# Chunk 4's transposes moved behind the first FFN product

## The chip, the cores and the metric

The kernel runs on one core of a Trainium2 chip. A core has five engines that run side by side, each with its own list of instructions: TensorE (PE, matrix products), VectorE (DVE), ScalarE (ACT), GpSimd (POOL) and SyncE (SP, which here only issues transfers). The metric is the device time of one execution in microseconds; lower is better. Before the change four runs took 779.92, 779.97, 781.87 and 782.6 us, median 780.92.

## What is computed

The reference applies attention with decay (no softmax) and then a feed-forward network with three up-projections:

```python
scores = scale * np.matmul(q, k.transpose(0, 1, 3, 2))     # 8 batches, 8 heads, 576 tokens, head size 64
gamma = 1.0 - 2.0 ** (-5.0 - np.arange(H))
Dmat = np.where(rel >= 0, gamma[:, None, None] ** rel[None, :, :], 0.0)
ret = np.matmul(scores * Dmat, v)                          # then x = ret as (4608, 512)
h = np.maximum(np.maximum(x @ w1, x @ w2), x @ w3)         # w1, w2, w3: 512 x 768
out = h @ w_out                                            # 768 x 512
```

q, k and v are float32. The four weight matrices arrive as 64-bit floats, and the kernel itself turns their bits into float32.

## The kernel before

**Attention.** The 4608 tokens are 36 chunks of 128. For each chunk `load` fetches k, q and v; `decay_values` (POOL) multiplies v by the key decay; `transposes` brings k and q into the layout that the scores need; `scores` forms the products and masks them (DVE); `state` forms k times v for the running state; `keep` adds it to the state (DVE) and decays it (POOL); `values` forms the chunk's output from the masked scores and the old state (L296, L309), and `output` scales it on DVE into xT, the FFN's input (L184 in the profile). `values` also forms its chunk's kv product (L260) where it has not been formed yet. For chunks 0 to 6 `transposes` uses TensorE (L229) and copies the two results, kT and qT, out of PSUM on ScalarE (L231); later chunks use VectorE.

**FFN.** Four chunks make a tile of 512 tokens (CPT = 4), and there are nine tiles. The hidden size 768 is six blocks of 128. In tile 0 the up-projections are plain: nine units, one for each pair of blocks and each of w1, w2, w3. A unit has two products of four matmuls (L600), one per block. The first matrix's product is copied into h on ScalarE (L604), the others are joined by a maximum on DVE (L603). The first unit's first product is called fb0 below, its second fb1. Later tiles use a scheme with fewer products, whose sums need VectorE.

**Weights.** The weights come in 24 pieces of 128 x 512 (512 KB each), pieces 0 and 1 for the first unit, 2 and 3 for the second, and so on. `load_weights` issues the transfers on SP; six buffers hold the raw bits, and each finished piece issues the load of another into its buffer. `convert_all` is a generator, and `convert(n)` moves it on by n steps. A piece has four: a mask on DVE (L486) and the low word on ScalarE (L487); two exponent steps on ScalarE (L489, L492) and a mask on DVE (L491); L497 on DVE; L502 and L508 on DVE, the last of which writes the float32 weights. L489 needs L486, and L502 needs L492. Pieces 0 and 1 are worked one by one, later ones in pairs: masks of both, then products of both.

**Order of the work.** Nothing plans the order; it is the order in which the program emits it. Each engine takes its instructions in that order, and an instruction that waits holds up all behind it on its engine. The first four chunks are emitted ahead of the FFN of tile 0, with conversion steps between them. Then, for each tile, the FFN generator `ffn(t)` and the attention steps of the following tile, `steps(t + 1)`, take turns: during tile 0, slot 0 loads chunk 5, the first unit follows, slot 1 emits chunk 4's scores, state and keep, the second unit follows, slot 2 emits chunk 5's transposes, and so on. PSUM banks come from three small pools; `ps_r` has four banks in rotation, used by scores, kv products, the outputs from chunk 3 on and the transposes of chunks 4 to 6.

Of the kernel before, what the change touches and what calls it, by code (L numbers as in the profile page):

```python
# [79 lines left out]
def kernel(  # L80
# [23 lines left out]
    CPT = NT // C  # L104
# [45 lines left out]
    def start_of(g):  # L150
        r = -g * C % S
        return r if r < C else None
# [8 lines left out]
    raws, vds, qks, sts, states, kvs = {}, {}, {}, {}, {}, {}  # L161
# [12 lines left out]
    def chore(n=1):  # L174
        for _ in range(n):
            if urgent or chores:
                (urgent or chores).popleft()()  # L177

    def soon(step):

        if spread:
            urgent.append(step)
        else:
            step()  # L184
# [24 lines left out]
    def decay_values(g):  # L209
        t = vds[g] = vpool.tile([C, H, D], FP32, tag="vd", name="vd")  # L210
        nc.gpsimd.tensor_tensor(t[:], raws.pop(("v", g))[:], gk[:].unsqueeze(2).to_broadcast([C, H, D]),  # L211
                                op=ALU.mult)

    def pair(t, p):
        return t[:, 2 * p:2 * p + 2, :].rearrange("a h d -> a (h d)")

    def transposes(g):
        both = qks[g] = {}
        if g >= BY_PE:
            for n in ("k", "q"):  # L220
                t = both[n] = att.tile([P, NP, C], FP32, tag=n + "T", name=n + "T", bufs=2 if n == "k" else 3)
                soon(partial(nc.vector.transpose, t[:].rearrange("a p c -> a (p c)"),
                             raws.pop(("kx" if n == "k" else n, g))[:].rearrange("a p b i -> a (p b i)")))
            return
        for n, src in (("k", raws["k", g]), ("q", raws.pop(("q", g)))):
            pool, tag = (ps_r, "r") if g >= CPT else (ps_x, "x")
            pt = pool.tile([P, NP, C], FP32, tag=tag, name=n + "t")
            for p in range(NP):
                nc.tensor.transpose(pt[:, p, :], pair(src, p), ident[:C, :C])  # L229
            t = both[n] = att.tile([P, NP, C], FP32, tag=n + "T", name=n + "T", bufs=2 if n == "k" else 3)  # L230
            nc.scalar.copy(t[:], pt[:])  # L231
# [14 lines left out]
    def begins(g):  # L246
        return g + 1 < NG and start_of(g + 1) != 0

    def half(j):
        return slice(D * j, D * (j + 1))  # L250
# [12 lines left out]
    def keep(g):  # L263
        def step(t, kv):
            if start_of(g) is not None:
                nc.vector.tensor_tensor(t[:], kv[:], gs[:], op=ALU.mult)
            else:
                nc.vector.tensor_tensor(t[:], kv[:], states[g][:], op=ALU.add)  # L268
                nc.gpsimd.tensor_tensor(t[:], t[:], gs[:], op=ALU.mult)  # L269

        if begins(g):
            t = states[g + 1] = stp.tile([P, NP, D], FP32, tag="state", name="state")
            soon(partial(step, t, kvs[g]))
# [3 lines left out]
    def head(c, n):  # L277

        return NP * c + n

    def values(chunks, new_states=(), later=False):

        def before(g):
            return C if start_of(g) is None else start_of(g)

        chore(len(urgent))
        t, i = divmod(chunks[0], CPT)
        pool, tag = (ps_r, "r") if chunks[0] >= CPT - 1 else (ps_y, "y")  # L290
        o = [pool.tile([P, len(chunks), NP // 2, C], FP32, tag=tag, name="o") for _ in range(2)]
        for m, g in enumerate(chunks):
            for n in range(NP):
                for c in range(2):
                    h = head(c, n)
                    nc.tensor.matmul(o[n % 2][half(c), m, n // 2, :], lhsT=vds[g][:, h, :],  # L296
                                     rhs=sts[g][:, h % 2, h // 2, :], start=m == 0 and n < 2,
                                     stop=before(g) == 0, skip_group_check=True)
        for g in new_states:
            if g not in kvs:  # L300
                state(g)
        for m, g in enumerate(chunks):
            old = before(g)
            if old > 0:
                for n in range(NP):
                    for c in range(2):
                        h = head(c, n)
                        r = half(h % 2)
                        nc.tensor.matmul(o[n % 2][half(c), m, n // 2, :old], lhsT=states[g][r, h // 2, :],  # L309
                                         rhs=qks[g]["q"][r, h // 2, :old], start=False, stop=True,  # L310
                                         skip_group_check=True)
        finish = partial(output, chunks, o, t, i)
        if later:
            return finish
        finish()
        for g in new_states[:1]:
            if g >= CPT:
                keep(g)
# [220 lines left out]
    def late_room():  # L539
        pool = late["pool"]  # L540
        late["W"] = [pool.tile([P, NF, P], FP32, name=f"n{n}") for n in range(1, 9)]
        late["X"] = {n: pool.tile([P, NH], FP32, name=n)[:] for n in sorted({x[0] for x in X_SUMS})}
# [3 lines left out]
    def convert(n):  # L546
        for _ in range(n):
            next(converting, None)
# [48 lines left out]
    def up_plain(t, h, fb, i):  # L597
        ps = (ps_x, ps_y)[fb % 2].tile([P, NT], FP32, tag="xy"[fb % 2], name="up")
        for dc in range(NDC):
            nc.tensor.matmul(ps[:], lhsT=w_sb[i, fb][:, dc * P:(dc + 1) * P], rhs=xT[t][:, dc, :],  # L600
                             start=(dc == 0), stop=(dc == NDC - 1))
        if i > 0:
            return lambda: nc.vector.tensor_tensor(h[:, fb, :], h[:, fb, :], ps[:], op=ALU.max)  # L603
        return lambda: nc.scalar.copy(h[:, fb, :], ps[:])  # L604

    def ffn(t):

        h = hpool.tile([P, NF, NT], FP32, tag="h", name="h")
        if t == 0:
            for fp, i in units:  # L610
                for fb in (2 * fp, 2 * fp + 1):
                    maximum = up_plain(t, h, fb, i)
                    convert(4)
                    maximum()
                yield
            convert(6)
            for fb, _ in enumerate(downs_plain(t, h)):
                convert(4 if fb < 2 else 4 * len(pieces))
                if fb == 2:
                    while_converting.close()  # L620
                    late["pool"] = ctx.enter_context(tc.tile_pool(name="late", bufs=1))
                    late_room()
                    sums_of_outs()
                elif fb > 2:
                    chore(2)
                if fb in (1, 3):
                    yield
            yield
            return
        if t == 1:  # L630
            spread.append(True)
            weight_sums(0)
            weight_sums(2)
        plain = (2, 3) if t == 1 else ()
        order = (2, 3, 0, 1, 4, 5) if t == 1 else (0, 1, 4, 5, 2, 3)
        total = sum(24 if fb in plain else len(PRODUCTS) for fb in order)
        count = parts = 0
        for n, fb in enumerate(order):
            if fb not in plain:
                while fb // 2 not in summed_fp:  # L640
                    chore()
            steps_of_one = up_plain_all(t, h, fb) if fb in plain else up(t, h, fb)
            for step, cost in enumerate(steps_of_one):
                if fb in plain:
                    chore(8)
                elif step % 2 or step % 5 == 4:
                    chore(len(urgent) > 0)
                elif step % 4 == 2 and chores:
                    chores.popleft()()
                count += cost or 1  # L650
                if count * (NF // 2 * 3) >= (parts + 1) * total:
                    parts += 1
                    yield
            if n % 2:
                sums_of_hidden(h, fb // 2)
                if fb in plain:
                    weight_sums(fb // 2)
        chore(len(urgent))
        for n, _ in enumerate(downs(t, h)):
            chore(4)  # L660
            if n in (1, 3):
                yield
        yield

    def up_plain_all(t, h, fb):
        for i in range(3):
            up_plain(t, h, fb, i)()
            yield 8
# [36 lines left out]
    keep(2)  # L705
    convert(2)
    values([2], [2])
    transposes(4)
    convert(2)
    decay_values(4)  # L710
    values([3], [3])
    keep(3)
    convert(4)

    def steps(t):

# [95 lines left out]
```

## Time and profile before

One execution was profiled.

| | before |
|---|---|
| median of four runs | 780.92 us |
| time of the profiled execution | 781.87 us |
| its span, first to last instruction | 780.2 us |
| PE busy | 768.6 us (99%) |
| DVE busy | 568.7 us (73%) |
| ACT busy | 325.9 us (42%) |
| POOL busy | 102.7 us (13%) |
| mean granted PE clock | 0.998 |

Span and time differ by 1.67 us, which lies outside the first and last instruction. Times in the views are microseconds from the start of the span. In a timeline a row gives the start, the length, the engine, the line of the kernel and the tiles written and read; neighbouring instructions of one kind are merged, and the square brackets show how long the engine was idle before and what ended that. PE's float32 matmuls appear as two records each. A busy share averages over stages: what counts for an edit in the first 40 us is which wait ends last there.

### The profile page before, as it was taken

What the parts mean: (1) busy time and instruction counts of PE and PEld (TensorE: products, weight loads), DVE (VectorE), ACT (ScalarE), POOL (GpSimd) and SP (SyncE); (2) the same over time, 40 slices, a digit from 0 to 9 for tenths busy, and PEclk for the clock granted to TensorE, in tenths of its full rate; (3) what the DMA queues carried; (4) which work ended last, traced back from release to release, by engine and by line L of the source; (5) the groups of instructions that cost most, each with busy time, mean ns of one, the idle gap of its engine ahead of it and who ended that gap; (6) DMA issues with size and microseconds to landing.
All of it is one profiled execution on the core that took longest, in us unless ns stands there. A gap on an engine that the chain in (4) does not pass through costs nothing.

```text
span 780.2 us, 14439 instructions
## 1 busy us (share of the span) xinstructions
PE 768.6 (99%) x5000; PEld 625.6 (80%) x5000; DVE 568.7 (73%) x1248; ACT 325.9 (42%) x808; POOL 102.7 (13%) x124
## 2 busy tenths in 40 slices
PE   8899999999999999999999999999999999999998
PEld 6545545588888888888888888888888888888887
DVE  2897998979667847786678767786778577855672
ACT  3565641144054513452345325441545054524651
POOL 3110112102011111111111111110012001200000
PEclk9999999999999999999999999999999999999999
DMA  9995643333223332333333333333333323001001
GB/s 211 244 233 128 165 103 95 57 58 58 74 45 72 68 66 63 58 61 64 85 55 58 56 97 59 57 58 96 58 55 57 75 55 68 15 14 42 2 1 54
DMA packets 236938, 59.33 MB, mean 76 GB/s; under 512 B 217920, under 2 KB 235584, under 8 KB 236864
## 3 DMA queue, kind: packets, MB, share of 16 engines
q1 hardware_dynamic: 236432, 58.14, 34.4%
q8 instruction: 39, 0.64, 0.4%
q14 instruction: 35, 0.29, 0.1%
q10 hardware_dynamic: 432, 0.27, 0.1%
HBM read 48.89 MB, written 9.44 MB: 75 GB/s over the span
## 4 chain that ended last, share of the span: by engine, by line
PE 93%; DVE 3%; DMA 2%; SPq 1%; issue 0%; ACT 0%; DVEq 0%; ACTq 0%
PE a L579 18%; PE b L579 15%; PE dx L424 11%; PE up L600 8%; PE c L579 8%; PE dz L424 5%; PE d L579 5%; PE e L579 5%; PE o L296 4%; PE s L240 4%; PE dy L424 3%; PE down L589 2%; PE o L309 2%; PE kv L260 2%; DVE w L344 1%; SPq L207 1%
## 5 line engine op out<-in xcount | busy, mean ns | idle before, releaser
L559 DVE TENSOR_TENSOR part<-part 128x256 f32<-128x256 f32 x460 | 211.0, 467 | 79.3 <-ACT part L564 71.3
L564 ACT COPY part<-a 128x256 f32<-128x256 f32 x276 | 102.7, 372 | 85.0 <-PE a L579 74.6
L564 ACT COPY part<-b 128x256 f32<-128x256 f32 x230 | 85.6, 372 | 125.8 <-PE b L579 114.0
L600 PE MATMUL up<-xT,w 128*128 128x512 f32 x192 | 84.5, 596 | 0.5 <-DVE xT L184 0.5
L211 POOL TENSOR_TENSOR vd<-vraw,gk 128x512 f32<-128x512 f32 x36 | 40.4, 1123 | 324.8 <-DMA vraw<-in_v_dram 167.8
L579 PE MATMUL a<-s,w 128*128 128x256 f32 x276 | 82.3, 380 | 0.0
L579 PE MATMUL b<-s,n 128*128 128x256 f32 x276 | 82.1, 379 | 0.0
L600 PEld LDWEIGHTS up<-xT,w 128*128 128x128 f32 x192 | 35.8, 190 | 43.6 <-issue 40.3
L579 PEld LDWEIGHTS b<-s,n 128*128 128x128 f32 x276 | 52.5, 190 | 7.1
L579 PEld LDWEIGHTS a<-s,w 128*128 128x128 f32 x276 | 52.3, 190 | 7.3 <-issue 0.2
L579 PE MATMUL c<-xT,w 128*128 128x256 f32 x184 | 56.0, 386 | 0.0
L579 PE MATMUL b<-xT,n 128*128 128x256 f32 x184 | 55.4, 383 | 0.0
L579 PE MATMUL d<-s,w 128*128 128x256 f32 x184 | 55.3, 382 | 0.0
L579 PE MATMUL a<-xT,n 128*128 128x256 f32 x184 | 47.2, 379 | 0.0
L579 PE MATMUL e<-xT,w 128*128 128x256 f32 x184 | 47.2, 379 | 0.0
L559 DVE TENSOR_TENSOR h<-part 128x256 f32<-128x256 f32 x92 | 41.5, 451 | 6.6
L424 PE MATMUL dx<-To,H 128*128 128x256 f32 x192 | 44.8, 383 | 0.0
L431 ACT COPY part<-dx 128x256 f32<-128x256 f32 x32 | 10.5, 375 | 80.0 <-PE dx L424 79.9
L177 DVE TENSOR_TENSOR xT<-o,gq 128x512 f32<-128x512 f32 x28 | 18.1, 686 | 33.5 <-PE o L309 33.5
L269 POOL TENSOR_TENSOR state<-state,gs 128x256 f32<-128x256 f32 x24 | 18.8, 784 | 171.8 <-DVE state L268 171.8
L424 PEld LDWEIGHTS dx<-To,H 128*128 128x128 f32 x192 | 35.9, 190 | 5.7 <-issue 1.0
L240 PEld LDWEIGHTS s<-qT,kT 64*128 64x128 f32 x576 | 33.7, 188 | 8.1 <-PE b L579 4.0
(104 smaller groups left out, 1301.2 us busy)
## 6 DMA issues: line engine op xcount, KB each, us to landing
bits<-in_moe_w_dram SPq DMA_DIRECT2D x36, 256.0 KB, 5.1
out_dram<-osb SPq DMA_DIRECT2D x35, 256.0 KB, 2.1
kraw<-in_k_dram SPq DMA_DIRECT2D x32, 256.0 KB, 3.0
vraw<-in_v_dram SPq DMA_DIRECT2D x32, 256.0 KB, 3.5
qraw<-in_q_dram SPq DMA_DIRECT2D x464, 16.0 KB, 1.9
kxraw<-in_k_dram SPq DMA_DIRECT2D x464, 16.0 KB, 1.8
bits<-in_moe_w_out_dram SPq DMA_DIRECT2D x6, 512.0 KB, 4.7
qraw<-in_q_dram SPq DMA_DIRECT2D x6, 256.0 KB, 4.5
```

The costliest lines, as they stand in the source:

```text
L177: (urgent or chores).popleft()()
L211: nc.gpsimd.tensor_tensor(t[:], raws.pop(("v", g))[:], gk[:].unsqueeze(2).to_broadcast([C, H, D]), op=ALU.mult)
L240: nc.tensor.matmul(s[j][:, p, :], lhsT=kT[r, p, :], rhs=qT[r, p, :], start=True, stop=True)
L260: nc.tensor.matmul(kvs[g][half(h % 2), h // 2, :], lhsT=kr[r:, h, :], rhs=vds[g][r:, h, :], start=True, stop=True)
L269: nc.gpsimd.tensor_tensor(t[:], t[:], gs[:], op=ALU.mult)
L296: nc.tensor.matmul(o[n % 2][half(c), m, n // 2, :], lhsT=vds[g][:, h, :], rhs=sts[g][:, h % 2, h // 2, :], start=m == 0 and n < 2, stop=be ...
L309: nc.tensor.matmul(o[n % 2][half(c), m, n // 2, :old], lhsT=states[g][r, h // 2, :], rhs=qks[g]["q"][r, h // 2, :old], start=False, stop=True,
L424: nc.tensor.matmul(out[m], lhsT=hS[n](fp)[:, m * P:(m + 1) * P], rhs=late["T"][n][:, fp, :], start=first and fp == 0 and (m == 0 or last a ...
L559: nc.vector.tensor_tensor(out, a, b, op=op)
L564: nc.scalar.copy(t[:], ps[step[0]][:])
L579: nc.tensor.matmul(ps[chain][:], lhsT=factor(w, fb), rhs=xS[t][x], start=n == 1, stop=ends, skip_group_check=True)
L600: nc.tensor.matmul(ps[:], lhsT=w_sb[i, fb][:, dc * P:(dc + 1) * P], rhs=xT[t][:, dc, :], start=(dc == 0), stop=(dc == NDC - 1))
```

## The change

In the opening part, chunk 4's transposes are no longer emitted between the outputs of chunks 2 and 3. They are emitted inside the first FFN unit, after fb0 and its copy into h; the conversion steps that stood ahead of that copy follow the transposes there. The opening part is put in another order too: chunk 3's output comes directly after chunk 2's, then the conversion of piece 1 (four steps), then chunk 3's `keep`, chunk 4's `decay_values` and the first two steps of pieces 2 and 3. The number of conversion steps is the same.

```diff
@@ ffn, tile 0
             for fp, i in units:
                 for fb in (2 * fp, 2 * fp + 1):
                     maximum = up_plain(t, h, fb, i)
+                    if CPT not in qks:
+                        maximum()
+                        transposes(CPT)
+                        convert(4)
+                        continue
                     convert(4)
                     maximum()
                 yield
@@ opening part
     keep(2)
     convert(2)
     values([2], [2])
-    transposes(4)
+    values([3], [3])
+    convert(4)
+    keep(3)
+    decay_values(CPT)
     convert(2)
-    decay_values(4)
-    values([3], [3])
-    keep(3)
-    convert(4)
```

`qks` holds the chunks whose transposes have been emitted, so the new branch is taken once, at fb0. On ScalarE the order of the instructions concerned was: chunk 4's two copies, the steps of pieces 1, 2 and 3, fb0's copy, piece 4. It becomes: the steps of pieces 1 and 2, fb0's copy, chunk 4's two copies, the steps of pieces 3 and 4. On PE chunk 4's eight transposes stand between fb0 and fb1. On POOL chunk 3's state product and chunk 4's decay change places. SP's transfers keep their order.

## The prediction

> **What bounds the kernel now.** I read the page first: busy shares, the 40 slices and the chain that ended last.
>
> ```profile
> span 780.2 us, 14439 instructions
> ...
> PE   8899999999999999999999999999999999999998
> DVE  2897998979667847786678767786778577855672
> ...
> PE 93%; DVE 3%; DMA 2%; SPq 1%; issue 0%; ACT 0%; DVEq 0%; ACTq 0%
> ```
>
> TensorE (PE) sets the end. It is short of work only in the first two slices (39 us; digits 8), and beyond them its timeline has one idle piece, 1.56 us at 153.57. So an edit gains only if PE's unbroken run starts earlier or holds less work. That run starts here (PE's timeline: start, length, engine, line; idle time and its releaser in brackets):
>
> ```profile
> 21.70 0.67 PE L309 MATMUL o<-qT,state 64*64 64x128 f32 x16
> 23.97 0.63 PE L229 MATMUL kt<-ident,kraw 128*128 128x128 f32 x4 [1.60 <-DMA kraw<-in_k_dram]
> 25.45 0.63 PE L229 MATMUL qt<-ident,qraw 128*128 128x128 f32 x4 [0.86 <-DVE expo L502]
> 26.01 1.82 PE L296 MATMUL o<-st,vd 128*64 128x128 f32 x16
> 27.61 1.08 PE L260 MATMUL kv<-vd,kraw 128*64 128x64 f32 x16
> 28.61 1.13 PE L309 MATMUL o<-qT,state 64*64 64x128 f32 x16
> 30.26 7.13 PE L600 MATMUL up<-xT,w 128*128 128x512 f32 x16 [0.51 <-DVE xT L184]
> 37.32 1.16 PE L240 MATMUL s<-qT,kT 64*128 64x128 f32 x16
> ```
>
> The 23.97 and 25.45 rows are chunk 4's transposes. Both wait for their loads. The second is put down to VectorE's L502, but the row of the DMA issues shows otherwise: q's second half was issued at 20.41 with 5.0 us to landing, 25.41. Chunk 3's output (o, kv, o) stands behind them in PE's order though nothing of chunk 4 enters it, and from 30.26 PE is full. On VectorE (DVE) and ScalarE (ACT):
>
> ```profile
> 23.59 1.22 DVE L502 SCALAR_TENSOR_TENSOR expo<-bits,expo 128x512 int32<-128x512 int32 x1
> 24.84 0.69 DVE L508 TENSOR_TENSOR w<-mant,expo 128x512 f32<-128x512 f32 x1
> 25.45 0.75 DVE L184 TENSOR_TENSOR xT<-o,gq 128x256 f32<-128x256 f32 x2
> 26.11 0.42 DVE L486 TENSOR_SCALAR expo<-bits 128x512 int32<-128x512 int32 x1
> ...
> 29.78 0.76 DVE L184 TENSOR_TENSOR xT<-o,gq 128x256 f32<-128x256 f32 x2 [2.92 <-PE o L309]
> ```
>
> ```profile
> 26.12 0.58 ACT L231 COPY qT<-qt 128x512 f32<-128x512 f32 x1 [0.90 <-PE qt L229]
> 26.60 0.77 ACT L487 ACTIVATE mant<-bits,one 128x512 f32<-128x512 uint32 x1
> ...
> 29.80 0.76 ACT L487 ACTIVATE mant<-bits,one 128x512 f32<-128x512 uint32 x1 [1.07 <-DMA bits<-in_moe_w_dram]
> ```
>
> DVE writes chunk 2's xT at 25.45 and stands idle 2.92 us before chunk 3's at 29.78. The last ACT row is piece 2, whose bits land at 29.8. The last view gives busy times and granted clock by stretch:
>
> ```profile
> 26.50:27.00 0.50, 0.50 (x10) 0.50 (x8) 0.36 (x2) 0.50 (x2) 0.31 (x1) 0.50 0.72 205
> 29.50:30.00 0.50, 0.24 (x8) 0.00 (x0) 0.22 (x1) 0.20 (x1) 0.00 (x0) 0.87 1.00 307
> ```
>
> The third number from the end is PE's clock: 0.50 from about 26.3 to 29.7, so chunk 3's output took 3.73 us (26.01 to 29.74) where chunk 2's kv, o, o took 2.16 (20.21 to 22.37).
>
> **What the Trainium skill says.** "TensorE: Matmul & The Clock Gate", Part 1: PE's clock is judged in free-running windows of about 3.4 us and halves after an idle one; Part 4 of that page: transposes do not count as busy in the same way. The trace agrees: between 22.37 and 26.01 there were only two transposes, and 3.4 us at 0.50 followed. Since the window is free-running, other runs need not have that stretch. The same page's table at the head: ACT and DVE take instructions strictly in order; here ACT's order is the program's, so what stands ahead of a copy delays it. "SBUF — State Buffer", Who interferes with whom: a DVE operation with two SBUF inputs and a GpSimd operation block each other; L502 took 1.22 us beside POOL's state product (23.15 to 24.25) and 0.69 without it.
>
> **The change, step by step.** Names: fb0 and fb1 are the first unit's two products (four matmuls each, 6.96 us for eight in later units, so 3.48); p0, p1, p2 ... the weight pieces.
>
> *PE up to fb0.* After chunk 2's output (22.37) comes chunk 3's. It needs the second masked scores (DVE, 22.74) and its last part needs the state from POOL (24.25), so at full clock it ends near 24.25 + 0.67 = 24.95. DVE, in order, has L502, L508 and chunk 2's xT first; chunk 3's xT takes the slot at 26.11 that p1's L486 has now. xT to fb0 was 30.26 - 29.78 = 0.48, so fb0 starts at 26.59: **3.67 us earlier**. p0 is ready at 25.53. PE waits about 1.6 us for this xT; DVE, not a load, is then the limit.
>
> *Transposes behind fb0.* They go into PE's full stretch. Chunk 5's pair shows the price there: 46.00 to 46.87, **0.87 us**. Their data landed at 25.4, their banks are free. fb1 starts at 26.59 + 3.48 + 0.87 = 30.94.
>
> *p1 (convert 4), for fb1.* DVE's L486 at 26.77, ACT's L489 at 27.22, L492 at 27.96 to 28.68, DVE's L502 28.71 to 29.40, L508 ends 30.12. fb1 needs it at 30.94: 0.8 us to spare, 0.3 if L502 takes 1.22.
>
> *The copies.* ACT's order becomes p1, p2, fb0's copy into h, kT, qT, p3. p2's first step waits for bits until 29.80; its L489 waits for DVE's L486, now behind chunk 3's state sum (30.04), so L486 is at 30.37, L489 at 30.82, L492 ends 32.28, h at 32.19 to 32.76, kT 32.65, qT 33.11 to 33.70. Chunk 4's scores are due at 30.94 + 3.48 = 34.42: hidden by fb1, 0.7 us to spare. Without that cover every microsecond would be PE's.
>
> *Pieces behind the copies.* p2 on DVE: L497 32.40, L508 ends 34.43; the next unit needs it at 34.42 + 1.71 (scores, kv) = 36.13. p3's ACT steps start only at 33.57 and end 35.69; L508 ends 37.13, needed 39.6. p4 ends 41.97, needed 43.97. So DVE comes forward by only some 1.3 to 2 us here, but its margin was 2.4 to 5 us and stays at 1.7 or more.
>
> *POOL and SP.* State product and decay of chunk 4 swap places; the decay ends near 32.4 instead of 27.8, needed by kv at 35.5. SP's list of DMAs keeps its order; p7's bits wait for p1's L502 (29.4, was 32.6) and leave up to 1.4 us earlier, chunk 5's loads behind them. No transfer moves later.
>
> *Sum.* 3.67 - 0.87 = 2.80 us. Later stages follow PE: DVE is idle 2.97 us before xT at 72.62 and 4.50 before the one at 120.47, both waiting for PE's o; the 1.56 us wait at 153.57 ends a DVE stretch that starts at 120.47, so it moves along. Span 780.2 - 2.8 = 777.4; time of that execution 781.87 - 2.80 = 779.07.
>
> *To the median.* The four runs are 779.92, 779.97, 781.87 (the profiled one) and 782.6. The half clock cost the profiled run 3.73 - 2.16 = 1.57 us. If the two short runs lacked it, they gain only 2.80 - 1.57 = 1.23 and the four become about 778.7, 778.7, 779.1, 779.8, median 778.9. If the spread has another cause, all gain 2.80: 780.92 - 2.80 = 778.1. I take the point between, **778.5**; the likeliest case's own range is 777.2 to 779.4.
>
> **Rivals.** (1) *The half clock moves onto fb0.* PE's new wait of 1.6 us and two short ones (some 0.5) leave the worst 3.4 us window a good 40% busy with matmuls. If that counts as idle, 3.4 us of products at half rate cost 1.7: 780.2. Against: 15.9 to 19.3, with 2.18 us busy, half of it transposes, kept the full clock. 0.06. (2) *Swallowed later*: pieces or the DVE stretch before 153.57 do not come forward and PE waits there instead: 780.9. For: DVE is full from 120 to 154; against: it starts when PE's o ends, and the margins above. 0.05. (3) *Slower: copies caught behind p2.* kT and qT now stand behind p2's steps. If its bits land later than 30.5, chunk 4's scores slip one for one; from 33.4 on nothing is gained, from 35.7 the kernel is over 0.3% slower, at 36 it would be some 783.5. For: DMA's share is about 1 there, and landings take up to 6.8 us; against: p2 was issued at 24.52 and 25.21, so it would have to take over 10. 0.06. That the edit does nothing (xT at 29.78 still) would need chunk 3's output to depend on chunk 4; it doesn't.
>
> **Numbers.** Forecast 0.83, rivals 0.06, 0.05, 0.06. A 0.3% bound (2.34 us, about what a measurement of this kernel can tell from no change) is 778.58. The forecast lies across it: 0.56 of its 0.83 below, since the span's gain of 2.80 is over it and only the clock's share pulls back; 0.27 within. Faster 0.56, same 0.27 + 0.06 + 0.05 = 0.38, slower 0.06. The range, 777.2 to 780.3, holds the forecast and rival 1 and leaves out the rest.
>
> **What would show it.** Right: PE's first L600 near 26.6 behind DVE's xT near 26.1; L229 for chunk 4 near 30.1 with no load wait; L240 near 34.5 with no idle time; clock full through 26 to 30; the wait near 150.8 still about 1.6. Wrong: idle time of PE before fb1 (p1), before L240 (copies), before the next unit (p2), or a clock of 0.50 at fb0.

## The result and the profile after

| | before | after |
|---|---|---|
| median, us | 781.18 | 779.38 |
| lowest to highest, us | 779.29 to 785.19 | 777.12 to 782.44 |
| profiled execution, us | 781.87 | 779.11 |
| its span, us | 780.2 | 777.4 |
| mean granted PE clock in it | 0.998 | 0.999 |

The ratio is 0.9974, with a 95% interval of 0.9966 to 0.9982: faster by 1.8 us at the medians. The two profiled executions differ by more, 2.8 us. The predicted time was 778.5; the range 777.2 to 780.3 holds the result. The likeliest of the three outcomes, a gain of more than 0.3%, did not come: the ratio's gain is 0.26%. What has to be explained is therefore not the sign but why 2.8 us in the traces become 1.8 or less in the medians.

First the page of the kernel after: span, the slices of PE and DVE, and the chain of work that ended last.

```profile
span 777.4 us, 14439 instructions
...
PE   8899999999999999999999999999999999999998
...
DVE  2998979889677857785769757876778567855672
...
PE 86%; DVE 6%; SPq 3%; DMA 3%; issue 1%; DVEq 0%; ACT 0%
```

PE is still full from the third slice on. The chain goes through DVE for 6% now (3% before), because PE's start hangs on DVE. PE's timeline of the kernel after shows where (start, length, engine, line; idle time before in brackets):

```profile
22.19 1.38 PE L296 MATMUL o<-st,vd 128*64 128x128 f32 x16 [0.60 <-DVE st L184]
23.40 0.63 PE L260 MATMUL kv<-vd,kraw 128*64 128x64 f32 x16
24.21 0.67 PE L309 MATMUL o<-qT,state 64*64 64x128 f32 x16 [0.18 <-POOL state L269]
26.48 3.70 PE L600 MATMUL up<-xT,w 128*128 128x512 f32 x8 [1.60 <-DVE xT L184]
30.02 0.60 PE L229 MATMUL kt<-ident,kraw 128*128 128x128 f32 x4
30.45 0.60 PE L229 MATMUL qt<-ident,qraw 128*128 128x128 f32 x4
30.89 3.60 PE L600 MATMUL up<-xT,w 128*128 128x512 f32 x8
34.42 1.16 PE L240 MATMUL s<-qT,kT 64*128 64x128 f32 x16
...
150.79 0.70 PE L579 MATMUL c<-s,w 128*128 128x256 f32 x2 [1.69 <-DVE h L603]
```

Chunk 3's output (22.19 to 24.88) waits for no load any more. fb0 starts at 26.48 instead of 30.26; behind it the transposes, fb1 and chunk 4's scores follow without idle time. The late wait moved from 153.57 to 150.79 and grew by only 0.13 us; in the kernel before its row was:

```profile
153.57 0.70 PE L579 MATMUL c<-s,w 128*128 128x256 f32 x2 [1.56 <-DVE h L603]
```

DVE and ScalarE of the kernel after, in the same stretch:

```profile
23.49 1.22 DVE L502 SCALAR_TENSOR_TENSOR expo<-bits,expo 128x512 int32<-128x512 int32 x1
24.74 0.69 DVE L508 TENSOR_TENSOR w<-mant,expo 128x512 f32<-128x512 f32 x1
25.35 1.41 DVE L184 TENSOR_TENSOR xT<-o,gq 128x256 f32<-128x256 f32 x4
26.68 0.41 DVE L486 TENSOR_SCALAR expo<-bits 128x512 int32<-128x512 int32 x1
...
29.36 0.69 DVE L508 TENSOR_TENSOR w<-mant,expo 128x512 f32<-128x512 f32 x1
...
30.64 0.95 DVE L491 TENSOR_SCALAR frac<-bits 128x512 int32<-128x512 int32 x1
31.51 1.26 DVE L486 TENSOR_SCALAR expo<-bits 128x512 int32<-128x512 int32 x1
...
34.35 0.69 DVE L508 TENSOR_TENSOR w<-mant,expo 128x512 f32<-128x512 f32 x1
```

```profile
28.91 0.78 ACT L487 ACTIVATE mant<-bits,one 128x512 f32<-128x512 uint32 x1 [0.31 <-DMA bits<-in_moe_w_dram]
...
32.13 0.57 ACT L604 COPY h<-up 128x512 f32<-128x512 f32 x1
32.60 0.59 ACT L231 COPY kT<-kt 128x512 f32<-128x512 f32 x1
33.08 0.60 ACT L231 COPY qT<-qt 128x512 f32<-128x512 f32 x1
```

The xT products of chunks 2 and 3 are one unbroken stretch now (25.35, four of them), and DVE's 2.92 us of waiting for PE are gone. qT is written by 33.68, 0.7 us ahead of the scores. In the stretches with clocks, the row that stood at 0.50 before stands at full clock here:

```profile
26.50:27.00 0.50, 0.50 (x1) 0.27 (x2) 0.50 (x2) 0.00 (x0) 0.00 (x0) 1.00 0.95 330
```

### The profile page after: what moved, and what is told of

Read it like the earlier page. It is cut to its first block, busy times and chain, and to the rows that moved or that the text cites. A ratio compares the mean times of both kernels' runs of the same rounds, so it can differ in the third digit from the quotient of the medians.

```text
span 777.4 us, 14439 instructions
## 1 busy us (share of the span) xinstructions
PE 766.6 (99%) x5000; PEld 623.6 (80%) x5000; DVE 570.3 (73%) x1248; ACT 325.8 (42%) x808; POOL 102.8 (13%) x124
## 4 chain that ended last, share of the span: by engine, by line
PE 86%; DVE 6%; SPq 3%; DMA 3%; issue 1%; DVEq 0%; ACT 0%
PE a L579 18%; PE b L579 15%; PE dx L424 11%; PE c L579 8%; PE dz L424 5%; PE d L579 5%; PE e L579 5%; PE up L600 5%; PE s L240 4%; PE o L296 4%; PE dy L424 3%; SPq L195 2%; PE kv L260 2%; PE o L309 2%; DMA bits<-in_moe_w_out_dram 1%; DVE w L344 1%
```

## The experiments

Besides the times I use the mean granted clock that every execution carries. Where a trace shows half clock, it holds for 3.41 us or twice that (five traces); one such stretch lowers the mean over 780 us by 3.41 x 0.5 / 780 = 0.0022. So executions sort into three groups: none (0.9985 and above), one stretch (0.9966 to 0.9985), more. The comparisons ran on several chips; each ratio is against the kernel before on its own chip, and medians of different chips are compared only with that in mind. The mean tells how many stretches an execution had, not where; the place is seen in a trace alone.

**The kernel after, again.**

> The changed kernel itself, once more beside the others, to have its clock in more executions. My theory (the half clock explains why the median gained less than the span): executions of the kernel before show a mean clock of 0.997 to 0.998 in about half of the cases and those are some 1.6 us longer; executions of this one show it in about a quarter, again some 1.7 us longer; where the clock is whole the two kernels differ by about 1.2 us, where the kernel before had the half clock and this one had not, by 2.8 us. Rival (the spread has another cause): the time does not follow the clock, and the difference is the same 1.8 us in every class. Span 777.4 us with the clock whole.

Measured: 779.77 us median of 22, ratio 0.9987 (0.9977 to 0.9998), a smaller gain than in the result, about 1 us. Its profiled execution has a span of 778.8. Its PE timeline, then its busy times by stretch (the third number from the end is the clock):

```profile
22.94 0.64 PE L260 MATMUL kv<-vd,kraw 128*64 128x64 f32 x16
23.75 0.67 PE L309 MATMUL o<-qT,state 64*64 64x128 f32 x16 [0.17 <-POOL state L269]
26.02 5.40 PE L600 MATMUL up<-xT,w 128*128 128x512 f32 x8 [1.60 <-DVE xT L184]
```

```profile
26.00:26.50 0.50, 0.48 (x1) 0.30 (x2) 0.50 (x2) 0.00 (x0) 0.00 (x0) 0.97 0.98 219
26.50:27.00 0.50, 0.50 (x2) 0.34 (x1) 0.46 (x2) 0.34 (x1) 0.00 (x0) 0.50 0.97 287
...
29.50:30.00 0.50, 0.50 (x2) 0.05 (x2) 0.50 (x3) 0.00 (x0) 0.00 (x1) 0.62 1.10 225
```

fb0 takes 5.40 us instead of 3.70: rival 1, the half clock on fb0, is real. It costs 1.70 us here. The groups, with all executions of the kernel before in three comparisons and of the kernel after in two (number, median us):

```
              none           one stretch     more
before (146)  44   779.5     82   780.9      20   783.6
after   (55)  37   779.1     17   780.5       1   782.4
```

Within a group the two kernels differ by only 0.4 us; they differ in how many executions fall into which. These sets mix chips, so the sum is made on the one chip that has clocks for both kernels (67 executions of before, 22 of after). There the group without half clock has medians of 779.63 and 779.12, the group with one stretch 780.99 and 780.52, and 41 of 67 executions of before have a stretch against 9 of 22 of after. Averaged over its executions, before loses (33 x 1.4 + 8 x 4.15) / 67 = 1.2 us to half clock, after 9 x 1.4 / 22 = 0.6. So of a mean gain of 1.0 us on that chip, some 0.6 is clock and 0.4 to 0.5 is order. On 22 executions the clock's part is uncertain: shares as far apart as 41 of 67 and 9 of 22 come by chance, to either side, in about one of seven such draws.

Of my expectation, the price of a stretch (1.4 us) held. The difference of 1.2 us where the clock is whole did not: it is 0.5. The share of the kernel after is nearer four in ten here than a quarter. The rival, one difference of 1.8 us in every group, fails too.

**The kernel before, again.**

> The kernel before itself, for a second trace of it. My theory: where the clock is whole, chunk 3's output takes about 2.2 us instead of 3.7, fb0 starts near 28.7 or earlier, and the time is near 779.6 us. If the difference of only 0.5 us between the two kernels' executions with the whole clock is a matter of selection (the clock stays whole when chunk 4's loads land early and TensorE's waits are short), the two waits ahead of L229 are together shorter than the 2.5 us of the first trace. Rival: with the whole clock the waits are as long as in the first trace and fb0 starts at 28.7.

Measured: 780.93, ratio 1.0004 (0.9993 to 1.0014). Its trace shows a different opening from the trace that I predicted from, and it is not the execution with a whole clock that I had hoped for. PE's timeline, then one stretch with its clock:

```profile
18.51 1.05 PE L229 MATMUL qt<-ident,qraw 128*128 128x128 f32 x4 [2.36 <-DMA qraw<-in_q_dram]
...
24.73 0.66 PE L229 MATMUL kt<-ident,kraw 128*128 128x128 f32 x4
25.23 0.60 PE L229 MATMUL qt<-ident,qraw 128*128 128x128 f32 x4
25.75 1.09 PE L296 MATMUL o<-st,vd 128*64 128x128 f32 x16
...
29.45 7.13 PE L600 MATMUL up<-xT,w 128*128 128x512 f32 x16 [1.54 <-DVE xT L184]
```

```profile
19.00:19.50 0.50, 0.50 (x5) 0.17 (x3) 0.00 (x0) 0.00 (x0) 0.07 (x1) 0.50 1.06 252
```

Chunk 3's q is late here (2.36 us), and the half clock follows that wait, before 22. By the time of chunk 4's transposes (24.73) the data are there, nothing waits, and fb0 is behind DVE, as it is in the kernel after. In such an execution there is no load wait for the change to take away. What it could gain and lose here can be estimated from the trace: without piece 1's masks ahead of it, chunk 3's xT could start at 28.13 on DVE instead of 28.99 (PE's o ends at 27.91), 0.86 us earlier, and the transposes behind fb0 would cost their 0.87. The half clock of this execution lies ahead of all that the change moves, so not every stretch in the groups above belongs to this place.

**One part alone: the transposes moved, the old order kept around them.**

```diff
# against before: the new branch in ffn, and
-    transposes(4)
```

> One part alone: the transposes go behind fb0, but the opening part keeps its old order, so that VectorE makes piece 1's two masks ahead of chunk 3's xT. My theory (fb0 starts when VectorE reaches chunk 3's xT): two instructions at 0.34 us stand ahead of it, xT starts 0.67 us later (26.7 instead of 26.0), fb0 at 27.15 instead of 26.48, span 778.0 us. Rival (the gain comes from taking the transposes' load waits off TensorE, the order of the rest is of no account): fb0 at 26.5, span 777.4 us. Piece 1 is ready before fb1 in both.

Measured: 781.75, ratio 1.0015 (1.0002 to 1.0027): slower than before. The timelines of DVE, POOL and PE:

```profile
25.13 0.75 DVE L184 TENSOR_TENSOR xT<-o,gq 128x256 f32<-128x256 f32 x2
25.79 1.28 DVE L486 TENSOR_SCALAR expo<-bits 128x512 int32<-128x512 int32 x1
26.99 0.42 DVE L491 TENSOR_SCALAR frac<-bits 128x512 int32<-128x512 int32 x1
27.33 0.74 DVE L184 TENSOR_TENSOR xT<-o,gq 128x256 f32<-128x256 f32 x2
```

```profile
25.74 1.04 POOL L211 TENSOR_TENSOR vd<-vraw,gk 128x512 f32<-128x512 f32 x1 [1.81 <-DMA vraw<-in_v_dram]
```

```profile
27.79 6.47 PE L600 MATMUL up<-xT,w 128*128 128x512 f32 x8 [3.14 <-DVE xT L184]
```

The two masks that stand ahead of chunk 3's xT in the old order keep it 1.54 us from its place (27.33 - 25.79). I had expected 0.67, from the trace of before, with 0.42 for each mask; here the first takes 1.28, beside `decay_values` on POOL (25.74 to 26.78). PE waits 3.14 us instead of 1.60. Two windows of 3.41 us at half clock follow, from 26.58 to 33.41 by the mean clocks at their ends (0.58 in 26.5 to 27.0, 0.59 in 33.0 to 33.5); fb0 lasts 6.47 us. PE was busy from 27.79 on, 2.20 us or 65% of the first of these windows, and the second came all the same. Fifteen of the 20 executions have a half-clock stretch; the five without have a median of 779.6, against 779.1 for the kernel after on this chip. Moving the transposes without moving the masks loses what it gains, in part by DVE's order and in part by the clock.

**The other part alone: the new order, transposes kept in the opening part, directly after chunk 3's output.**

```diff
# against after: no branch in ffn, and
     values([3], [3])
+    transposes(4)
     convert(4)
```

> One part alone: the opening part in its new order, but the transposes stand directly behind chunk 3's output and not behind fb0; their banks are those of the changed kernel's pool, and their copies stand ahead of piece 1's steps on ScalarE. My theory: q's transposes take the bank of chunk 3's output and wait for its xT, so fb0 starts 0.4 us later than in the changed kernel; qT's copy pushes piece 1's steps back on ScalarE, piece 1 is ready some 0.7 us after fb0 has ended and TensorE waits for it ahead of fb1; against that the 0.87 us of the transposes are gone from the full stretch. With the whole clock that is +0.4 + 0.7 - 0.87 = 0.2 us over the changed kernel, 779.3 us. Rival (taking the transposes out of the FFN stretch is a clear gain wherever they stand): no wait ahead of fb1 and 778.2 us, as with the transposes in the gap.

Measured: 779.16 (20 executions), ratio 0.9982 (0.9976 to 0.9988), only one of the 20 with a half-clock stretch. PE's timeline:

```profile
26.84 0.66 PE L229 MATMUL qt<-ident,qraw 128*128 128x128 f32 x4 [1.01 <-DVE xT L184]
27.33 3.60 PE L600 MATMUL up<-xT,w 128*128 128x512 f32 x8
31.65 3.70 PE L600 MATMUL up<-xT,w 128*128 128x512 f32 x8 [0.72 <-DVE w L508]
```

The second transpose waits for a PSUM bank that xT still reads, its copy delays piece 1 on ScalarE, and fb1 waits 0.72 us for that piece. Even so its ratio lies between the two ratios of the kernel after (0.9974 and 0.9987): the gain doesn't need the place behind fb0. What the two versions have in common is chunk 3's output ahead of the transposes and its xT ahead of piece 1's masks; in the run before, which had only the first, there was no gain. By its trace it is 0.50 us behind the kernel after at chunk 4's scores (the table below); that it has fewer stretches of half clock may make up for that, but the two ran on different chips.

**Transposes inside PE's wait, with banks of another pool.** To take away both waits of that version, piece 1's masks go ahead and the banks come from the pool of the earlier chunks.

```diff
# against after: no branch in ffn, and
     values([3], [3])
-    convert(4)
+    convert(1)
+    transposes(4)
+    convert(3)
# in transposes
-            pool, tag = (ps_r, "r") if g >= CPT else (ps_x, "x")
+            pool, tag = (ps_r, "r") if g > CPT else (ps_x, "x")
```

> The transposes stand directly behind chunk 3's output, in the time in which TensorE waits for xT in the changed kernel (24.9 to 26.5), with banks from the pool of the earlier transposes so that they need not wait for xT; piece 1's two masks are emitted ahead of their copies on ScalarE. My theory (fb0's start is set by VectorE, TensorE is idle 1.6 us before it, and the transposes cost 0.87 us only because they stand in its full stretch): L229 at 24.9 and 25.4, fb0 still at 26.5, fb1 at 30.0 with a wait of about 0.1 us for piece 1, span 776.6 us, 0.8 us less than the changed kernel. Rival (the loads of chunk 4 or the copies on ScalarE get in the way): fb0 or fb1 starts 0.5 us or more later than that and the span is 777.2 us or more.

Measured: 778.45 (22 executions), ratio 0.9970 (0.9961 to 0.9980), on the chip where the kernel after had 0.9987. Without half clock it takes 778.2, the kernel after 779.1 on that chip. Its PE timeline:

```profile
23.67 0.66 PE L229 MATMUL kt<-ident,kraw 128*128 128x128 f32 x4
24.17 0.60 PE L229 MATMUL qt<-ident,qraw 128*128 128x128 f32 x4
25.44 7.24 PE L600 MATMUL up<-xT,w 128*128 128x512 f32 x16 [0.67 <-ACT qT L231]
32.60 1.16 PE L240 MATMUL s<-qT,kT 64*128 64x128 f32 x16
```

The transposes take up most of the wait that the kernel after spends idle, so their 0.87 us leave PE's full stretch. What is left of the wait, 0.67 us, is put down to the copy of qT. This version beats both kernels.

**The copies' place on ScalarE.** The conversion steps of pieces 2 and 3 go ahead of fb0's copy and chunk 4's copies:

```diff
                     if CPT not in qks:
+                        convert(4)
                         maximum()
                         transposes(CPT)
-                        convert(4)
                         continue
```

> One part undone: on ScalarE fb0's copy and chunk 4's two copies stand behind the three steps of piece 3 instead of ahead of them; TensorE's and VectorE's orders are those of the changed kernel. My theory (ScalarE takes instructions in order and only fb1 covers the copies, with 0.7 us to spare): kT is copied at 34.7 and qT ends at 35.7, chunk 4's scores start at 35.8 instead of 34.4, TensorE is idle 1.3 us ahead of them, span 778.7 us. Rival (the place of the copies is of no account, the gain is all in chunk 3's output): no idle time ahead of L240, span 777.4 us.

Measured: 780.30 (12 executions), ratio 0.9999 (0.9986 to 1.0012). The profiled execution does not show the wait ahead of the scores, because its fb0 ran at half clock (5.40 us) and so gave the copies 1.7 us more; that trace settles nothing on its own. The six executions without half clock have a median of 780.1 us, 1.0 more than the kernel after on the same chip. To see the wait itself, the same order was run again, with six products of the identity that nobody reads put on PE behind chunk 3's output, to keep the clock up:

```diff
     values([3], [3])
+    fill_pe(6)
```

`fill_pe(n)` emits n products of the identity with itself into a bank of `ps_x`.

> The copies behind piece 3's steps on ScalarE, as in the earlier run of that order, now with six extra products of the identity (read by nobody) in TensorE's wait ahead of fb0, so that the clock stays whole and fb0 keeps its 3.5 us. My theory (ScalarE's order matters because only fb1 covers the copies; in the earlier trace the half clock lengthened fb0 by 1.7 us and hid the loss): TensorE is idle 1.3 us ahead of chunk 4's scores, released by qT's copy, and executions with the whole clock take 1.0 to 1.3 us more than the 778.5 us of the changed kernel with its wait filled: about 779.7 us. Rival (the copies' place is of no account): no idle time there and 778.6 us.

Measured: 780.11 (20 executions), ratio 0.9991 (0.9983 to 0.9998). Its PE timeline, then ScalarE's:

```profile
30.59 3.60 PE L605 MATMUL up<-xT,w 128*128 128x512 f32 x8
35.49 1.16 PE L245 MATMUL s<-qT,kT 64*128 64x128 f32 x16 [1.30 <-ACT qT L236]
```

```profile
34.84 0.60 ACT L236 COPY qT<-qt 128x512 f32<-128x512 f32 x1
```

Now PE waits 1.30 us for qT at the scores. In the group without half clock this version takes 780.0; the same filled kernel with the copies in the change's place (next) takes 778.5. The two ran on different chips, where the kernel before has the same 779.3 in that group.

**The wait before fb0 filled**, in the kernel after (the same six products, the rest as it is):

> The changed kernel with six extra products of the identity with itself (their result is read by nobody) on TensorE in the time in which it waits for chunk 3's xT, and nothing else changed. My theory (that wait of 1.6 us is what lets the clock drop to a half in 9 of 22 executions, at 1.4 us each): the half clock is seen in at most 3 of 22, executions with the whole clock stay at 779.1 us, the median comes to about 779.1 us. Rival (the drop comes from somewhere else, or the fillers delay fb0): the share of executions with the half clock stays near 4 in 10 and the median at 779.8 us, or fb0 starts later than 0.1 us after xT.

Measured: 778.71 (15 executions), ratio 0.9967 (0.9954 to 0.9981); three of 15 with a half-clock stretch. Its PE timeline:

```profile
24.83 1.60 PE L153 MATMUL fillps<-ident 128*128 128x128 f32 x12
26.51 3.70 PE L605 MATMUL up<-xT,w 128*128 128x512 f32 x8
```

fb0 starts where it did (26.51), so the products cost nothing in that wait. Three of 15 against 18 of 55 alone tells little (a difference of that size, to either side, comes by chance in about one of two such draws). With the copies' pair added it is clearer: a half-clock stretch in 4 of 35 executions filled, in 24 of 67 not filled (about 1 in 100 by chance). This adding up of two kernels and several chips was made after the results were known, so it supports the expectation without settling it.

**The waits of the kernel before filled:** six products ahead of `transposes(4)`, three between its two halves.

> The kernel before with extra products of the identity (read by nobody) on TensorE in its two waits for chunk 4's loads: six ahead of the first transposes and three between the two. My theory (those waits let the clock drop to a half in 41 of 67 executions): the half clock is seen in at most a quarter, and the median falls by about 1 us, to the 779.6 us of the executions with the whole clock; TensorE's order and waits are otherwise the same, so the changed kernel with its wait filled should be faster than this one only by what the order is worth, between 0.5 us (the difference of the two kernels' executions with the whole clock) and the 1.2 us of my sum. Rival (the clock is not the cause of the spread): no change, 780.6 us.

Measured: 779.69 (14 executions), ratio 0.9991 (0.9983 to 0.9999); one of 14 with a half-clock stretch, where the kernel before has 39 of 52 on this chip (102 of 146 on three). This shows that it is PE's idle time at these waits that lets the clock drop. Without moving anything, 0.7 us by the ratio (1.2 by the medians) come back. PE's timeline:

```profile
23.26 0.63 PE L234 MATMUL kt<-ident,kraw 128*128 128x128 f32 x4 [0.81 <-DMA kraw<-in_k_dram]
...
27.60 7.13 PE L607 MATMUL up<-xT,w 128*128 128x512 f32 x16 [0.52 <-DVE xT L189]
```

The three products between the halves last 0.83 us, which may or may not have been spent waiting for q anyway. They may well have cost something: in the group without half clock this version takes 779.7, the kernel before without them 779.3 on the same chip, though those may be the executions whose loads came early. So against the filled kernel after (778.5 without half clock, the same chip) the difference of 1.2 us is the worth of the order, less up to 0.83.

**The version with the transposes in the wait, filled as well:** two products ahead of chunk 3's output, two behind the transposes.

> The transposes in the gap ahead of fb0, as in the earlier run of that order, with two extra products of the identity (read by nobody) ahead of chunk 3's output and two behind the transposes. My theory (the 0.6 and 0.7 us waits that are left there let the clock drop in 5 of 22 executions): the half clock is seen in at most 1 or 2 of 22, the median falls by 0.2 to 0.3 us to 778.2 us, executions with the whole clock stay at 778.2 us. Rival (the drops that are left come from earlier waits, for the loads of chunks 2 and 3, as in the second trace of the kernel before): the share and the median of 778.5 us stay as they were. In both cases it beats the kernel before by 0.3% and the changed one by 0.1% or more.

Measured: 778.36 (7 executions), ratio 0.9971 (0.9960 to 0.9983), none with half clock. Whether the products help here stays open: without them five of 22 have a stretch, but the medians are alike.

**One measure for all traces.** Loads land at different times, so starts are not comparable as they stand. The mask is only a rough zero point, since DVE may reach it late: in "before, again" it stands directly behind chunk 2's score masks, which waited for PE. From piece 0's first mask on DVE (L486 before any insertion; the first row of its kind) to chunk 4's scores on PE the traces give, in us:

```
                                       mask    scores  between
before, predicted from                20.78    37.32   16.54  (1.57 of it half clock)
before, again                         22.81    36.52   13.71
before, filled                        20.42    34.66   14.24
after                                 20.68    34.42   13.74
after, again (fb0 at half clock)      20.22    35.65   15.43
after, filled                         20.70    34.45   13.75
copies last, filled                   20.38    35.49   15.11
new order, transposes kept            21.04    35.28   14.24
transposes moved alone                20.46    38.51   18.05  (2.77 of it half clock)
copies last (fb0 at half clock)       21.11    36.55   15.44
transposes in the wait                19.54    32.60   13.06
transposes in the wait, filled        20.64    33.94   13.30
```

The kernel after repeats to 0.01 us but for the clock. The kernel before ranges over 2.8 us, of which 1.57 is half clock and the rest, as I read it, the lateness of what it waits for. The transposes moved alone lose, beyond the clock, 18.05 - 2.77 - 13.74 = 1.54 us to the kernel after, which is just the time of the two masks. At half clock copies last and the kernel after are equal (15.44 and 15.43): the longer fb0 covers the copies.

## Why the prediction was right, and where not

**PE up to fb0, right.** fb0 was to start at 26.59 behind DVE's xT and started at 26.48, after a wait of 1.60 (about 1.6). The run with the transposes moved alone shows that the masks' place ahead of xT is part of this step, and that the 0.67 us expected for them there was too little: 1.54 with POOL beside them. (Chunk 3's output was to end at 24.95, where 24.25 + 0.67 makes 24.92; it ended at 24.88, and nothing hung on it.) "SBUF — State Buffer", Who interferes with whom, in the Trainium skill, says that DVE's `tensor_scalar` can enter a mode that contends with GpSimd for a shared port pair; the masks are of this kind, and 0.42 against 1.28 us agrees. So do the ends: the slow mask ends at 27.07, 0.29 us after POOL's instruction (26.78), and in the kernel after the two slow masks end 0.29 and 0.28 us after POOL's (31.59 after 31.30, 32.77 after 32.49). In the first 160 us of all twelve traces every mask of over 0.45 us (57 of them) is one that began while an instruction of POOL was running, and it ends 0.27 to 0.31 us after that instruction; no mask that began so kept its 0.42. A mask that began before POOL's instruction (30.30 against 30.46) did.

**Transposes at 0.87, right** (30.02 to 30.89), and the version with the transposes in the wait shows that this was a price for the place: without half clock it is 0.9 us faster.

**Piece 1, the copies, the scores, right.** Piece 1 was ready at 30.05 (30.12), qT written at 33.68 (33.70), scores at 34.42 (34.42). The 0.7 us of cover was the true margin: with the two pieces' steps ahead, the scores waited 1.30.

**Pieces behind the copies, right with one miss.** Piece 2 was ready at 35.04, not 34.43: the masks at 30.64 and 31.51 took 0.95 and 1.26 us beside POOL's state product (30.46 to 31.30) and decay (31.27 to 32.49), where the sum has some 0.4 for each. It was needed at 36.12, so nothing followed. Piece 3 was ready at 37.16 (37.13) and piece 4 at 41.96 (41.97).

**The sum, right for the execution it was made for.** 2.80 us, span 777.4, time 779.07 against 779.11; the table too has 16.54 - 13.74 = 2.80.

**To the median: the step that failed.** I took the point between two cases. One was that all executions gain 2.80; it is refuted: "before, again" is, by the measure above, no later at the scores than the kernel after, and at this place has nothing to gain (0.86 against 0.87 us). The other was that the executions without half clock gain 2.80 - 1.57 = 1.23, which made 778.9. It is nearer, but its term was mis-sized too: measured by groups it is 0.4 to 0.5 us, and against the filled kernel before at most 1.2. The reason is in the traces: 3.67 - 1.57 = 2.10 us is what the loads of chunk 4 and DVE's wait cost beyond the clock in one execution. By the measure of all traces, the filled kernel before loses only 0.50 to the kernel after, "before, again" nothing. How often which lateness occurs can't be read from three traces; the group medians suggest that it is small in most. That the range holds the result is in part luck: at 779.38 it lies at the very end of the likeliest case's own range (777.2 to 779.4), and the second comparison's ratio, 0.9987, would put the median of 781.18 at 780.2, which lies in the range only because it reached to rival 1.

**Rival 1 was put wrong.** I gave 0.06 to "the half clock moves onto fb0", as if it were true of all executions or none. It is a share: 18 of 55 executions of the kernel after have such a stretch somewhere, and two traces (the kernel after again, and copies last) show it on fb0, at the 1.7 us that the rival named. In how many of the 18 it is on fb0 is not shown. Such executions lie within the range because it reached to this rival. My argument against it, a stretch from 15.9 to 19.3 with 2.18 us busy at full clock, was about one position of a free-running window. In the execution that lost it, half clock held from 26.47 to 29.88 (the half-microsecond stretches at its two ends have mean clocks of 0.97 and 0.62), and the 3.41 us before 26.47 held kv's end, o and the start of fb0, 0.52 + 0.67 + 0.45 = 1.64 us or 48% busy. In the Trainium skill, "TensorE: Matmul & The Clock Gate", the table of Why this matters for your kernels, asks for no PE gaps over some 3 us; here a gap of 1.60 us with one of 0.17 before it was enough in this execution, and the measurement decides. It doesn't give the busy share below which the clock drops: with the same wait the trace of the first comparison kept the full clock.

**Rival 2, swallowed later, is refuted**: the wait at 150.79 is 1.69 against 1.56, and PE's list of waits holds no new one behind it. **Rival 3, copies behind late bits, did not occur**: piece 2's step waited for its bits to 28.91, earlier than the 29.80 that the sum used. That late copies do cost PE's time one for one is shown by copies last, filled: there the copy of qT starts 14.46 us after the first mask, in the kernel after 12.40, which is 2.06 us later; less the 0.7 of cover this leaves 1.3, and PE waited 1.30.

What stays open: why the two comparisons of the kernel after differ (0.9974 and 0.9987, intervals just overlapping), and why the filled kernel after is 0.6 us below the unfilled one even in the group without half clock; they ran on different chips, and before's own group median there is 0.3 lower. How much of the gain is clock and how much is order is known only roughly for the same reason: the kernel after and its filled version, and the two kernels filled and unfilled, were not all run on one chip.

## What to carry to other kernels

When a load wait is removed, ask in how many executions it is that late: one trace gives one arrival, and a gain worked out against a wait for a transfer is an upper estimate until a second trace of the same kernel confirms it. Where the last wait is on another engine, put PE's movable work into that wait rather than into its full stretch; that was worth another 0.9 us here. A half-clock stretch is a share of executions, not a yes or no: weigh it by the idle time in the worst window, and test it with products that nobody reads.

## What was not expected of the hardware

- A PE wait of 1.60 us, with PE busy for 48% of the 3.41 us before the drop, was followed by 3.41 us at half clock (26.47 to 29.88). In another run a window at half clock with PE busy for 65% of it was followed by a second one. A stretch costs 1.4 us in the medians of the times, 1.7 in a trace.
- Six identity products in the wait ahead of fb0 did not delay it (26.51 against 26.48). Nine such products in the waits of the kernel before brought the executions with half clock from 39 of 52 to 1 of 14, on the same chip.
- DVE's masks of 128 x 512 words took 0.42 us alone. Where an instruction of POOL had begun first they took 0.57 to 1.30 us, and all 57 of them ended 0.27 to 0.31 us after it: the mask seems to do its work only when POOL's instruction is over.
- Chunk 4's loads, 2.5 us of waiting in one execution of the kernel before, cost nothing in another, while there chunk 3's q was waited for 2.36 us.
